# Cached attention on one core: two K blocks to the transposing DMA, a new list of K blocks turned by VectorE, and the first query projection in two row halves

## The chip, the cores and the metric

The kernel runs on one core of a Trainium2 chip. The metric is device time in microseconds (us) of one execution; the median over the executions shown is what is compared. Engines are named as the profile names them: PE (TensorE matmuls), PEld (its weight loads), DVE (VectorE), ACT (ScalarE), POOL (GpSimd), SP (the queue that issues most transfers).

## The reference, cut to what matters

```python
B, Sq, D = 8, 32, 1024;  Hq, Hkv, Sk, Dh = 32, 4, 8192, 128      # all bf16
W, rep = 2048, 8                                                  # W = Sk // 4; rep = Hq // Hkv
q = (x @ wq).reshape(B, Sq, Hq, Dh).transpose(0, 2, 1, 3)
k = repeat(k_cache[:, :, Sk-W:, :], rep, axis=1);  v likewise
p = softmax(einsum("bhqd,bhkd->bhqk", q, k) * Dh**-0.5)
out = einsum("bhqk,bhkd->bhqd", p, v).transpose(0, 2, 1, 3).reshape(B, Sq, Hq*Dh) @ wo
```

Only the last 2048 positions of the cache are used. There are 4 groups of 8 query heads; a group shares one K and one V of each batch row.

## The kernel before, in words

**Units and slots.** The work is 32 *units*, one for each pair of group and batch row, group by group: unit u is group u // 8 and batch row u % 8. A unit has 256 query rows (8 heads of 32 rows) against 2048 keys. It is done in four *slots* of 512 keys, so slot s belongs to unit s // 4, and there are 128 slots. In a slot PE makes the scores of this slot (`s_ps`, 4 matmuls of 256 columns), then the product with V of the slot two before (`o_ps`, 8 matmuls of 129 columns; the last of the 129 sums the softmax's denominator), and then whatever side work is planned for the slot. ACT takes the exponential of each slot's scores (`pT`) in one instruction. PE's stream is in exactly this order, so a score matmul that has to wait holds back all that stands behind it.

**Side work of PE.** It is put into slots by `side_plan`: the query projection of groups 1 to 3 (`q_pieces`, 16 pieces of 4 matmuls of 256 columns for each group, spread over `Q_SLOTS`), the output projection (`o_pieces`, over `O_SLOTS`), and, for the units in `PE_T`, the turning of K (`k_pieces`: 16 PE transposes of 128x128 for a unit, 4 in each slot of the unit before). The projection of group 0 is done in `start`, before the first score: for the first `Q_CUT` = 6 of the 8 pieces of the contraction on all 256 rows, for the last two on 128 rows; the other 128 rows of those two follow in slots 0 and 1 (`q_rest`). The pieces of `q_pieces` and of `k_pieces` share the two PSUM buffers of `ps_m`.

**Three ways to turn K.** The scores need K with the head dimension on the partitions. Units in `PE_T` (0 to 4) load K as it is and turn it on PE, with a copy out of PSUM by DVE. Units in `V_T` load K as it is (`k_raw`), DVE turns it in blocks of 32x32 (`kb`, four instructions), and then sixteen moves of blocks put it in place (`kTv`), all by POOL, except for unit 5, where DVE makes four of them. A score matmul of such a unit reads what all sixteen moves have written. All other units load K by a transposing DMA in two halves (`kT`, 256 KB each). An entry of `V_T` gives the unit in whose `load_unit` the load is issued, the slots of the four DVE blocks, and the first and last slot over which the moves are spread:

```python
V_T = {5: (2, (5, 6, 8, 10), 10, 17, 12),
       **{u: (u - 4, range(4 * u - 16, 4 * u - 12), 4 * u - 13, 4 * u - 4, 16) for u in (8, 11, 14, 17, 20, 23, 26, 29)}}
```

**Loads.** Nearly every transfer is issued by SP, in the order of `load_unit`, into one queue: for a unit the first half of K, V, the second half of K, and then the raw K of a later unit and the weights that `W_AT` assigns. Units 0 to 3 are issued in `start`, 4 to 7 at slot 8, unit u from 8 on at slot 4(u - 5). These slots only order the stream: SP itself waits for buffers and for room in the queue, not for slots. DVE also works in program order: at a unit's start it copies V beside the column of ones (`va_copy`, L409), two slots into the next unit it normalises the last one's result and turns it (`finish_unit`: L415, L420, L422), and it makes the casts of the query pieces (L278) and the blocks of `V_T` (L251) where the plan puts them. The raw K of `V_T` units is in four buffers, the turned K of those units in two (`kvt`, shared with the raw K of units 0 and 1), `kb` in two, V in six.

Of the kernel before, what the change touches and what calls it, by code (L numbers as in the profile page):

```python
# [11 lines left out]
BF16 = mybir.dt.bfloat16  # L12
FP32 = mybir.dt.float32
# [2 lines left out]

RL_LIMIT = 1.0e22
RL_MIN = 1.0e-10
Q_CUT = 6
N_WARM = (8, 0, 0)  # L20
VA_ROW = 160
V_HALVES = 30

PE_T = (0, 1, 2, 3, 4)

V_T = {5: (2, (5, 6, 8, 10), 10, 17, 12),
       **{u: (u - 4, range(4 * u - 16, 4 * u - 12), 4 * u - 13, 4 * u - 4, 16) for u in (8, 11, 14, 17, 20, 23, 26, 29)}}
W_AT = (3, 3, 4, 4, 8, 8, 9, 9, 11, 12, 13, 13, 14, 15, 16, 16, 18, 19, 19, 20, 22, 22, 23, 24, 25, 26, 28, 28)

Q_SLOTS = {1: (17, 31), 2: (38, 54), 3: (69, 83)}  # L30
O_SLOTS = {0: (54, 71), 1: (84, 101), 2: (99, 123), 3: (124, 143)}


# [71 lines left out]
class Fast:  # L105
# [101 lines left out]
    def load_unit(self, ui):  # L207

        if ui < len(self.units):
            if ui not in V_T:  # L210
                self.load_k(ui, None if ui in PE_T else 0)
            self.load_v(ui, self.nc.sync)
            if ui not in V_T and ui not in PE_T:
                self.load_k(ui, 1)
        for u, at in V_T.items():
            if at[0] == ui:
                self.load_k(u)
        for p, at in zip(self.weights, W_AT):
            if at == ui:
                p()  # L220

    def k_pieces(self, ui):

        if ui not in PE_T:
            return []
# [39 lines left out]
    def q_pieces(self, g):  # L267
        nc, P, DC = self.nc, self.P, self.DC
        st = {}

        def piece(hl, i):
            if i == 0:
                st["ps"] = self.ps_m.tile([P, 512], FP32, name="q_ps", tag="m")
            for c in range(i * DC // 2, (i + 1) * DC // 2):
                nc.tensor.matmul(st["ps"][:, 0:self.NQ], lhsT=self.wq_t[g, i][:, c % (DC // 2), hl * P:(hl + 1) * P],  # L275
                                 rhs=self.xT[:, c, :], start=(c == 0), stop=(c == DC - 1))
            if i == 1:
                nc.vector.tensor_copy(out=self.q_view(g)[:, :, hl, :],  # L278
                                      in_=st["ps"][:, 0:self.NQ].rearrange("p (b s) -> p b s", b=self.B))
        return [lambda h=h, i=i: piece(h, i) for h in range(self.rep) for i in range(2)]  # L280

    def o_pieces(self, g, t, cuts=(512, 512), st=None):

# [28 lines left out]
    def start(self):  # L312
        nc, P = self.nc, self.P
        warm = self.ps_s.tile([P, 512], FP32, name="warm_ps", tag="s_ps")
        one = nc.const_aps.tensor
        x_sb = self.vp.tile([P, self.NT, self.D], BF16, name="x_sb", tag="v")
        xf = self.x.rearrange("b s d -> (b s) d")
        H = self.DC // 2

        nc.sync.dma_start(out=x_sb[:, 0, :], in_=xf[0:P, :])  # L320
        nc.scalar.dma_start(out=x_sb[:, 1, :], in_=xf[P:2 * P, :])
        wq0 = self.load_wq(0, 0, (1, 1, 1, 1)) + self.load_wq(0, 1, (2, 1, 1))
        for p in wq0[:5]:
            p()
        self.load_k(0, 0)
        wq0[5]()
        wq0[6]()
        self.load_k(0, 1)
        self.load_v(0, nc.sync)
        self.load_k(1)  # L330
        self.load_v(1, nc.sync)
        self.weights = []
        for g in range(self.Hkv):
            if g + 1 < self.Hkv:
                self.weights += self.load_wq(g + 1, 0) + self.load_wq(g + 1, 1)
            if g:
                self.weights += self.load_wo(2 * g - 2) + self.load_wo(2 * g - 1)
        self.weights += self.load_wo(2 * self.Hkv - 2) + self.load_wo(2 * self.Hkv - 1)
        for ui in range(2, 4):
            self.load_unit(ui)  # L340
        for v in self.va:
            nc.gpsimd.memset(v[:, :, self.Dh:self.VW], 1.0)
        nc.gpsimd.memset(self.ones_c[:, :], 1.0)
        def warm_up(n):
            for i in range(n):
                nc.tensor.matmul(warm[:, :], lhsT=one(1.0, [P, P], BF16), rhs=one(1.0, [P, 512], BF16), start=True, stop=True)
        warm_up(N_WARM[0])


        def x_turn(half, pl, tag):  # L350
            ps = pl.tile([P, H, self.NT, P], BF16, name="xT_ps", tag=tag)
            for c in range(H):
                for t in range(self.NT):
                    nc.tensor.transpose(ps[:, c, t, :], x_sb[:, t, half * H + c:self.D:self.DC], self.ident[:, :])
            for i, copy in ((0, nc.vector.tensor_copy), (1, nc.scalar.copy)):
                c0 = half * H + i * H // 2
                copy(out=self.xT[:, c0:c0 + H // 2, :], in_=ps[:, i * H // 2:(i + 1) * H // 2, :, :].rearrange("p c t s -> p c (t s)"))

        x_turn(0, self.ps_m, "m")
        x_turn(1, self.ps_s, "s_ps")  # L360
        qs = [pl.tile([P, 2, self.NQ], FP32, name="q0_ps", tag=tag)
              for pl, tag in ((self.ps_o, "o_ps"), (self.ps_o, "o_ps"), (self.ps_m, "m"), (self.ps_m, "m"))]
        KT = self.KT
        tp = None

        def k_turn(half):
            for j in range(half * KT // 2, (half + 1) * KT // 2):
                nc.tensor.transpose(tp[:, j, :], self.k_raw[0][:, j, :], self.ident[:, :])

        def k_copy(half):  # L370
            sl = slice(half * KT // 2, (half + 1) * KT // 2)
            nc.vector.tensor_copy(out=self.kT[0][:, sl, :], in_=tp[:, sl, :])

        def q_mm(c, h, n0, n1):
            nc.tensor.matmul(qs[h // 2][:, h % 2, n0:n1], lhsT=self.wq_t[0, c // H][:, c % H, h * P:(h + 1) * P],  # L375
                             rhs=self.xT[:, c, n0:n1], start=(c == 0 and h % 2 == 0), stop=(c == self.DC - 1),
                             skip_group_check=True)

        for c in range(self.DC):
            for h in range(self.rep):  # L380
                q_mm(c, h, 0, P if c >= Q_CUT else self.NQ)
            if c == 0:
                warm_up(N_WARM[2])
                warm_sb = self.c1.tile([P, 8], BF16, name="warm_sb")
                nc.vector.tensor_copy(out=warm_sb[:, :], in_=warm[:, 0:8])
            if c == self.DC - 3:
                tp = self.ps_s.tile([P, KT, P], BF16, name="kf_ps", tag="s_ps")
                k_turn(0)
                k_copy(0)
        k_turn(1)  # L390

        def q_copy(eng, k, b0, b1):
            src = qs[k][:, :, :].rearrange("p h (b s) -> p b h s", b=self.B)[:, b0:b1, :, :]
            dst = self.q_view(0)[:, b0:b1, k * 2:(k + 1) * 2, :]
            (nc.vector.tensor_copy if eng == "v" else nc.scalar.copy)(out=dst, in_=src)
        for k, eng in ((0, "a"), (1, "v"), (2, "a"), (3, "v")):
            q_copy(eng, k, 0, 1)
        k_copy(1)
        self.va_copy(0)

        def q_rest(k):
            for h in (2 * k, 2 * k + 1):
                for c in range(Q_CUT, self.DC):
                    q_mm(c, h, P, self.NQ)
            q_copy("v", k, 1, self.B)
        self.q_rest = [lambda k=k: q_rest(k) for k in (0, 2, 3, 1)]

    def va_copy(self, ui):
        self.nc.vector.tensor_copy(out=self.va[ui % 3][:, :, 0:self.Dh], in_=self.v_sb[ui][:, :, :])  # L409
# [16 lines left out]
    def side_plan(self):  # L426

        S = self.B * self.NCH
        plan = {s: [] for s in range((len(self.units) + 8) * self.NCH)}

        def spread(pieces, s0, s1):
            for k, p in enumerate(pieces):
                plan[s0 + (s1 - s0) * k // len(pieces)].append(p)
        for g, w in Q_SLOTS.items():
            spread(self.q_pieces(g), *w)
        for g, w in O_SLOTS.items():
            spread(self.o_pieces(g, 0) + (self.o_pieces(g, 1) if g < self.Hkv - 1 else []), *w)
        for ui, (_, s0, s1, s2, _) in V_T.items():
            blocks, moves = self.kv_pieces(ui)
            for k, p in enumerate(blocks):  # L440
                plan[s0[k]].append(p)
            spread(moves, s1, s2)
        return plan

    def run(self):
        nc, P, NCH, CJ, UQ, QT_N, KT = self.nc, self.P, self.NCH, self.CJ, self.UQ, self.QT_N, self.KT
        self.start()
        plan = self.side_plan()
        for i, p in enumerate(self.q_rest):
            plan[i // 2].append(p)  # L450
        pv_queue = []

        loads = {8: [4, 5, 6, 7], **{4 * (u - 5): [u] for u in range(8, len(self.units))}}
# [202 lines left out]
```

## Time and profile before

| what | value |
|---|---|
| median of 14 runs | 185.96 us (185.38 to 187.82) |
| the profiled execution | 185.7 us, of which its span is 183.6 us and 2.1 us lie around it |
| first score matmul | 12.74 us after the span's start |
| last exponential ends | 174.4 us |
| PE busy / DVE / ACT / POOL | 97% / 63% / 72% / 52% of the span |
| DMA: read from HBM | 41.4 MB |
| granted PE clock | full throughout |

Times in this text count from the start of the profiled span. The page gives for each engine its busy time, and a row of digits for 40 equal slices of the span (4.6 us each), where 9 means a slice busy to 90% or more. A timeline view lists instructions in order of time, neighbours of one kind put together (x8), with the time from the first one's start to the last one's end; matmuls overlap, so a group's time is longer than the distance to the next group, and it is the distance that counts.

### The profile page before, as it was taken

To read this page: it belongs to the slowest core of one execution; us is meant where nothing else is said; L and a number is where in the kernel's file an instruction comes from. 1 tells how busy PE (TensorE), PEld (TensorE's weight loads), DVE (VectorE), ACT (ScalarE), POOL (GpSimd) and SP (SyncE) were. 2 spreads that over 40 slices of the span, in tenths; PEclk is the share of its full clock that TensorE was granted. 3 is DMA by queue.
4 is the path that set the end of the run, shared out by engine and by line. 5 is a ranking of instruction groups with operands and counts; after the bars stand their busy time and mean duration, and the time that the engine had idled before them with its cause. 6 is when DMAs were issued, how large, how long until landed. Compare 5 with 4: busy or idle time off the path is not lost.

```text
span 183.6 us, 5041 instructions
## 1 busy us (share of the span) xinstructions
PE 178.9 (97%) x2041; PEld 153.6 (84%) x2057; DVE 115.5 (63%) x266; ACT 131.6 (72%) x133; POOL 95.0 (52%) x150
## 2 busy tenths in 40 slices
PE   8999999999999999999999999999999999999994
PEld 2899989999999999987878999988787888888843
DVE  0248799996585785685557558647755865365363
ACT  2218898777889787878787677787877888888800
POOL 2000019749939959929954980796299279600000
PEclk9999999999999999999999999999999999999999
DMA  6999999899998989999999999999999999960003
GB/s 192 341 404 409 399 402 379 125 276 385 258 355 264 347 289 326 400 253 255 365 366 241 374 398 239 241 345 385 245 369 335 209 284 291 225 172 0 0 29 93
DMA packets 52953, 51.72 MB, mean 282 GB/s; under 512 B 39744, under 2 KB 40256, under 8 KB 52928
## 3 DMA queue, kind: packets, MB, share of 16 engines
q1 hardware_dynamic: 52352, 50.90, 97.5%
q10 hardware_dynamic: 576, 0.49, 0.8%
q8 instruction: 15, 0.25, 0.5%
q14 instruction: 10, 0.08, 0.1%
HBM read 41.42 MB, written 0.52 MB: 228 GB/s over the span
## 4 chain that ended last, share of the span: by engine, by line
PE 83%; DMA 14%; SPq 1%; issue 1%; DVE 0%
PE o_ps L478 29%; PE s_ps L467 28%; PE op_ps L295 14%; PE q_ps L275 11%; DMA k_raw<-in_k_cache_dram 6%; DMA v_sb<-in_v_cache_dram 5%; DMA wq_sb<-in_wq_dram 3%; SPq L164 1%; PE tp L236 1%; SPq L320 0%; DVE o_t L305 0%; PE cnt_ps L532 0%
## 5 line engine op out<-in xcount | busy, mean ns | idle before, releaser
L469 ACT ACTIVATE pT<-s_ps 128x1024 bf16<-128x1024 f32 x128 | 128.8, 1025 | 33.0 <-PE s_ps L467 32.1
L261 POOL TENSOR_SCALAR kTv<-kb 32x512 bf16<-32x512 bf16 x140 | 94.1, 672 | 64.0 <-PE s_ps L467 34.6
L478 PE MATMUL o_ps<-va,pT 128*128 128x129 bf16 x1024 | 78.8, 220 | 0.1
L478 PEld LDWEIGHTS <-pT 128*128 128x128 bf16 x1024 | 68.5, 98 | 3.1
L467 PE MATMUL s_ps<-QT,kT 128*128 128x256 bf16 x368 | 55.2, 272 | 0.2
L467 PEld LDWEIGHTS <-kT 128*128 128x128 bf16 x368 | 34.8, 98 | 10.3
L295 PE MATMUL op_ps<-wo_sb,OT 128*128 128x512 bf16 (+2 forms) x128 | 32.7, 352 | 0.6
L275 PE MATMUL q_ps<-xT,wq_sb 128*128 128x256 bf16 x192 | 28.2, 273 | 0.0
L409 DVE COPY va<-v_sb 128x2048 bf16<-128x2048 bf16 x32 | 25.4, 795 | 0.1
L251 DVE STREAM_TRANSPOSE kb<-k_raw 128x512 bf16<-128x512 bf16 x36 | 23.8, 685 | 0.0
L415 DVE RECIPROCAL RL_all<-o_ps 128x2 f32<-128x2 f32 x32 | 5.3, 165 | 28.0 <-PE o_ps L478 27.9
L467 PE MATMUL s_ps<-QT,kTv 128*128 128x256 bf16 x144 | 21.6, 272 | 0.0
L420 DVE TENSOR_SCALAR o_sb<-o_ps,RL_all 128x128 bf16<-128x128 f32 x64 | 19.5, 347 | 1.1
L467 PEld LDWEIGHTS <-kTv 128*128 128x128 bf16 x144 | 13.9, 98 | 5.1
L275 PEld LDWEIGHTS <-wq_sb 128*128 128x128 bf16 x192 | 17.0, 98 | 1.2
L278 DVE CAST QT<-q_ps 128x256 bf16<-128x256 f32 x24 | 9.8, 407 | 12.8 <-PE q_ps L275 12.8
L422 DVE STREAM_TRANSPOSE OT<-o_sb 128x256 bf16<-128x256 bf16 x32 | 14.3, 446 | 1.1
L295 PEld LDWEIGHTS <-OT 128*128 128x128 bf16 x144 | 11.4, 98 | 2.3 <-DVE OT L422 0.2
L302 DVE TENSOR_TENSOR oacc<-op_ps,oacc 128x512 f32<-128x512 f32 x8 | 5.5, 682 | 7.4 <-PE op_ps L295 7.4
L375 PE MATMUL q_ps<-xT,wq_sb 128*128 128x256 bf16 (+1 forms) x80 | 7.7, 251 | 0.0
L375 PEld LDWEIGHTS <-wq_sb 128*128 128x128 bf16 x80 | 6.6, 98 | 0.9 <-issue 0.2
L236 PE MATMUL tp<-ident,k_raw 128*128 128x128 bf16 x64 | 5.9, 219 | 0.2 <-DMA k_raw<-in_k_cache_dram 0.2
(30 smaller groups left out, 36.8 us busy)
## 6 DMA issues: line engine op xcount, KB each, us to landing
v_sb<-in_v_cache_dram SPq DMA_DIRECT2D x30, 512.0 KB, 7.2
wo_sb<-in_wo_dram SPq DMA_DIRECT2D x16, 512.0 KB, 6.3
wq_sb<-in_wq_dram SPq DMA_DIRECT2D x13, 512.0 KB, 7.3
k_raw<-in_k_cache_dram SPq DMA_DIRECT2D x13, 512.0 KB, 5.7
wq_sb<-in_wq_dram SPq DMA_DIRECT2D x6, 256.0 KB, 5.0
v_sb<-in_v_cache_dram SPq DMA_DIRECT2D x4, 256.0 KB, 5.0
kT<-in_k_cache_dram SPq DMA_TRANSPOSE x36, 6.6
k_raw<-in_k_cache_dram SPq DMA_DIRECT2D x2, 256.0 KB, 6.4
```

Of the source, the lines that this page charges most:

```text
L251: nc.vector.transpose(out=st["kb"][:, sl, :], in_=self.k_raw[ui][:, sl, :])
L261: nc.gpsimd.tensor_scalar(out=out, in0=in_, scalar1=1.0, scalar2=1.0, op0=ALU.mult, op1=ALU.mult)
L275: nc.tensor.matmul(st["ps"][:, 0:self.NQ], lhsT=self.wq_t[g, i][:, c % (DC // 2), hl * P:(hl + 1) * P], rhs=self.xT[:, c, :], start=(c == ...
L278: nc.vector.tensor_copy(out=self.q_view(g)[:, :, hl, :], in_=st["ps"][:, 0:self.NQ].rearrange("p (b s) -> p b s", b=self.B))
L295: nc.tensor.matmul(ps[:, 0:w], lhsT=self.OT[:, gq, c, t * P:(t + 1) * P], rhs=self.wo_t[gq][:, c, n0:n0 + w], start=(k == 0), stop=(k == 7))
L375: nc.tensor.matmul(qs[h // 2][:, h % 2, n0:n1], lhsT=self.wq_t[0, c // H][:, c % H, h * P:(h + 1) * P], rhs=self.xT[:, c, n0:n1], start=(c ...
L409: self.nc.vector.tensor_copy(out=self.va[ui % 3][:, :, 0:self.Dh], in_=self.v_sb[ui][:, :, :])
L420: nc.vector.tensor_scalar(out=o_sb[:, qt, :, :], in0=o_ps[:, qt, 0:Dh].rearrange("p (i c) -> p c i", c=4), scalar1=rl[:, ui * QT_N + qt:ui ...
L422: nc.vector.transpose(out=self.OT[:, g * QT_N:(g + 1) * QT_N, :, b * self.Sq:(b + 1) * self.Sq], in_=o_sb[:, :, :, :])
L467: nc.tensor.matmul(s_ps[:, jj, :], lhsT=self.kT[ui][:, c * CJ + jj, :], rhs=q_u, start=True, stop=True)
L469: nc.scalar.activation(out=pT[:, :, :], in_=s_ps[:, :, :], func=ACT.Exp, bias=0.0, scale=self.scale)
L478: nc.tensor.matmul(o_ps[:, qt, 0:self.VW], lhsT=pT[:, jj, qt * P:(qt + 1) * P], rhs=va[:, j, 0:self.VW], start=(j == 0 and qt == 0), stop= ...
```

## The change

Units 3 and 4 leave `PE_T`; their K comes by transposing DMA. `V_T` now has units 5, 9, 11, 13, 16, 18, 21, 23, 26 and 29 in place of 5, 8, 11, 14, 17, 20, 23, 26 and 29. So 19 units use the transposing DMA in place of 18, 13 load raw K in place of 14. In `load_unit` the weights now come ahead of the raw K of a later unit. In the projection of group 0, heads 0 to 3 are done on all 256 rows before the first score, heads 4 to 7 on the first 128 rows only; the second 128 rows of these four heads are done by `q_late`, two heads in slots 0 and 1, two in slots 8 and 10. The first turn of K0 on PE moves behind the sixth of the eight contraction pieces. The projection of group 1 starts in slot 14 in place of 17 (one piece in each of the slots 14 to 29), four heads at a time on their first half of the contraction and then on their second. In all later groups two heads share one PSUM buffer and one cast.

```diff
-PE_T = (0, 1, 2, 3, 4)
+PE_T = (0, 1, 2)
 V_T = {5: (2, (5, 6, 8, 10), 10, 17, 12),
-       **{u: (u - 4, range(4 * u - 16, 4 * u - 12), 4 * u - 13, 4 * u - 4, 16) for u in (8, 11, 14, 17, 20, 23, 26, 29)}}
+       9: (5, range(21, 25), 24, 32, 16),
+       **{u: (u - 4, range(4 * u - 16, 4 * u - 12), 4 * u - 13, 4 * u - 4, 16) for u in (11, 13, 16, 18, 21, 23, 26, 29)}}
-Q_SLOTS = {1: (17, 31), 2: (38, 54), 3: (69, 83)}
+Q_LATE = {0: (0, 2), 1: (8, 12)}
+Q_SLOTS = {1: (14, 31), 2: (38, 54), 3: (69, 83)}
...
     def load_unit(self, ui):
...
+        for p, at in zip(self.weights, W_AT):
+            if at == ui:
+                p()
         for u, at in V_T.items():
             if at[0] == ui:
                 self.load_k(u)
-        for p, at in zip(self.weights, W_AT):
-            if at == ui:
-                p()
...
     def q_pieces(self, g):
...
+        n = 4 if g == 1 else 2
+        return [lambda h=h, i=i: piece(h, i) for h0 in range(0, self.rep, n) for i in range(2) for h in range(h0, h0 + n)]
+
+    def q_late(self, h0):
...
+            for c in range(DC):
+                nc.tensor.matmul(st["ps"][:, i, :], lhsT=self.wq_t[0, c // (DC // 2)][:, c % (DC // 2), (h0 + i) * P:(h0 + i + 1) * P],
+                                 rhs=self.xT[:, c, P:self.NQ], start=(c == 0 and i == 0), stop=(c == DC - 1), skip_group_check=True)
             if i == 1:
+                nc.vector.tensor_copy(out=self.q_view(0)[:, B // 2:, h0:h0 + 2, :].rearrange("p b h s -> p h b s"),
+                                      in_=st["ps"][:, :, :].rearrange("p h (b s) -> p h b s", b=B // 2))
...
-        def q_mm(c, h, n0, n1):
+        def q_mm(c, h):
+            ps, n = (qs[h // 2][:, h % 2, :], self.NQ) if h < 4 else (qs[2][:, h - 4, :], P)
...
         for c in range(self.DC):
-            for h in range(self.rep):
-                q_mm(c, h, 0, P if c >= Q_CUT else self.NQ)
...
-            if c == self.DC - 3:
+            if c == self.DC - 2:
                 tp = self.ps_s.tile([P, KT, P], BF16, name="kf_ps", tag="s_ps")
                 k_turn(0)
                 k_copy(0)
+            for h in range(self.rep):
+                q_mm(c, h)
...
-        for i, p in enumerate(self.q_rest):
-            plan[i // 2].append(p)
```

More of the change, by code (lines that the diff above doesn't have):

```diff
@@ L18 @@
 RL_MIN = 1.0e-10
-Q_CUT = 6
-N_WARM = (8, 0, 0)
+N_WARM = 8
 VA_ROW = 160
 V_HALVES = 30
-PE_T = (0, 1, 2, 3, 4)
+PE_T = (0, 1, 2)
 V_T = {5: (2, (5, 6, 8, 10), 10, 17, 12),
-       **{u: (u - 4, range(4 * u - 16, 4 * u - 12), 4 * u - 13, 4 * u - 4, 16) for u in (8, 11, 14, 17, 20, 23, 26, 29)}}
+       9: (5, range(21, 25), 24, 32, 16),
+       **{u: (u - 4, range(4 * u - 16, 4 * u - 12), 4 * u - 13, 4 * u - 4, 16) for u in (11, 13, 16, 18, 21, 23, 26, 29)}}
 W_AT = (3, 3, 4, 4, 8, 8, 9, 9, 11, 12, 13, 13, 14, 15, 16, 16, 18, 19, 19, 20, 22, 22, 23, 24, 25, 26, 28, 28)
-Q_SLOTS = {1: (17, 31), 2: (38, 54), 3: (69, 83)}
+Q_LATE = {0: (0, 2), 1: (8, 12)}
+Q_SLOTS = {1: (14, 31), 2: (38, 54), 3: (69, 83)}
 O_SLOTS = {0: (54, 71), 1: (84, 101), 2: (99, 123), 3: (124, 143)}
@@ L271, in piece @@
         def piece(hl, i):
+            k = hl // 2
+            if i == 0 and hl % 2 == 0:
+                st[k] = self.ps_m.tile([P, 2, self.NQ], FP32, name="q_ps", tag="m")
+            for c in range(i * DC // 2, (i + 1) * DC // 2):
+                nc.tensor.matmul(st[k][:, hl % 2, :], lhsT=self.wq_t[g, i][:, c % (DC // 2), hl * P:(hl + 1) * P],
+                                 rhs=self.xT[:, c, :], start=(c == 0 and hl % 2 == 0), stop=(c == DC - 1), skip_group_check=True)
+            if i == 1 and hl % 2 == 1:
+                nc.vector.tensor_copy(out=self.q_view(g)[:, :, 2 * k:2 * k + 2, :].rearrange("p b h s -> p h b s"),
+                                      in_=st[k][:, :, :].rearrange("p h (b s) -> p h b s", b=self.B))
@@ L272, in piece @@
+        n = 4 if g == 1 else 2
+        return [lambda h=h, i=i: piece(h, i) for h0 in range(0, self.rep, n) for i in range(2) for h in range(h0, h0 + n)]
+    def q_late(self, h0):
+        nc, P, DC, B = self.nc, self.P, self.DC, self.B
+        st = {}
+        def piece(i):
             if i == 0:
[L273 to L276, printed above, removed]
+                st["ps"] = self.ps_m.tile([P, 2, P], FP32, name="ql_ps", tag="m")
+            for c in range(DC):
+                nc.tensor.matmul(st["ps"][:, i, :], lhsT=self.wq_t[0, c // (DC // 2)][:, c % (DC // 2), (h0 + i) * P:(h0 + i + 1) * P],
+                                 rhs=self.xT[:, c, P:self.NQ], start=(c == 0 and i == 0), stop=(c == DC - 1), skip_group_check=True)
@@ L277, in piece @@
             if i == 1:
-                nc.vector.tensor_copy(out=self.q_view(g)[:, :, hl, :],
-                                      in_=st["ps"][:, 0:self.NQ].rearrange("p (b s) -> p b s", b=self.B))
-        return [lambda h=h, i=i: piece(h, i) for h in range(self.rep) for i in range(2)]
+                nc.vector.tensor_copy(out=self.q_view(0)[:, B // 2:, h0:h0 + 2, :].rearrange("p b h s -> p h b s"),
+                                      in_=st["ps"][:, :, :].rearrange("p h (b s) -> p h b s", b=B // 2))
@@ L282, in o_pieces @@
+        return [lambda i=i: piece(i) for i in range(2)]
     def o_pieces(self, g, t, cuts=(512, 512), st=None):
@@ L346, in warm_up @@
                 nc.tensor.matmul(warm[:, :], lhsT=one(1.0, [P, P], BF16), rhs=one(1.0, [P, 512], BF16), start=True, stop=True)
-        warm_up(N_WARM[0])
+        warm_up(N_WARM)
         def x_turn(half, pl, tag):
@@ L360, in start @@
         x_turn(1, self.ps_s, "s_ps")
-        qs = [pl.tile([P, 2, self.NQ], FP32, name="q0_ps", tag=tag)
-              for pl, tag in ((self.ps_o, "o_ps"), (self.ps_o, "o_ps"), (self.ps_m, "m"), (self.ps_m, "m"))]
+        qs = [self.ps_o.tile([P, 2, self.NQ], FP32, name="q0_ps", tag="o_ps") for _ in range(2)]
+        qs.append(self.ps_m.tile([P, 4, P], FP32, name="q0_ps", tag="m"))
         KT = self.KT
@@ L372, in k_copy, with q_copy @@
             nc.vector.tensor_copy(out=self.kT[0][:, sl, :], in_=tp[:, sl, :])
-        def q_mm(c, h, n0, n1):
-            nc.tensor.matmul(qs[h // 2][:, h % 2, n0:n1], lhsT=self.wq_t[0, c // H][:, c % H, h * P:(h + 1) * P],
-                             rhs=self.xT[:, c, n0:n1], start=(c == 0 and h % 2 == 0), stop=(c == self.DC - 1),
+        def q_mm(c, h):
+            ps, n = (qs[h // 2][:, h % 2, :], self.NQ) if h < 4 else (qs[2][:, h - 4, :], P)
+            nc.tensor.matmul(ps, lhsT=self.wq_t[0, c // H][:, c % H, h * P:(h + 1) * P],
+                             rhs=self.xT[:, c, 0:n], start=(c == 0 and h in (0, 2, 4)), stop=(c == self.DC - 1),
                              skip_group_check=True)
+        def q_copy(copy, h0, h1, b0, b1):
+            ps = qs[h0 // 2] if h0 < 4 else qs[2]
+            copy(out=self.q_view(0)[:, b0:b1, h0:h1, :].rearrange("p b h s -> p h b s"),
+                 in_=ps[:, :, b0 * self.Sq:b1 * self.Sq].rearrange("p h (b s) -> p h b s", s=self.Sq))
         for c in range(self.DC):
-            for h in range(self.rep):
-                q_mm(c, h, 0, P if c >= Q_CUT else self.NQ)
[L382 to L385, printed above, removed]
-            if c == self.DC - 3:
+            if c == self.DC - 2:
                 tp = self.ps_s.tile([P, KT, P], BF16, name="kf_ps", tag="s_ps")
@@ L389, in start @@
                 k_copy(0)
-        k_turn(1)
[L392 to L397, printed above, removed]
+            for h in range(self.rep):
+                q_mm(c, h)
+            if c == 0:
+                warm_sb = self.c1.tile([P, 8], BF16, name="warm_sb")
+                nc.vector.tensor_copy(out=warm_sb[:, :], in_=warm[:, 0:8])
+        k_turn(1)
+        q_copy(nc.scalar.copy, 0, 2, 0, 1)
+        q_copy(nc.vector.tensor_copy, 2, 4, 0, 1)
+        q_copy(nc.scalar.copy, 4, 8, 0, 1)
         k_copy(1)
         self.va_copy(0)
[L401 to L406, printed above, removed]
+        q_copy(nc.vector.tensor_copy, 0, 2, 1, self.B)
+        q_copy(nc.vector.tensor_copy, 2, 4, 1, self.B)
+        q_copy(nc.vector.tensor_copy, 4, 8, 1, self.B // 2)
     def va_copy(self, ui):
@@ L433, in spread @@
                 plan[s0 + (s1 - s0) * k // len(pieces)].append(p)
+        for k, w in Q_LATE.items():
+            spread(self.q_late(4 + 2 * k), *w)
         for g, w in Q_SLOTS.items():
```

## The prediction

> **What bounds the kernel now.** I read the page's first part, the rows of its second part, the chain, and then timelines of single engines.
>
> ```profile
> PE 178.9 (97%) x2041; PEld 153.6 (84%) x2057; DVE 115.5 (63%) x266; ACT 131.6 (72%) x133; POOL 95.0 (52%) x150
> ...
> DMA  6999999899998989999999999999999999960003
> ...
> PE 83%; DMA 14%; SPq 1%; issue 1%; DVE 0%
> ...
> L261 POOL TENSOR_SCALAR kTv<-kb 32x512 bf16<-32x512 bf16 x140 | 94.1, 672 | 64.0 <-PE s_ps L467 34.6
> ```
>
> PE never rests, and the chain is PE but for the first 28 us; side work taken from PE should therefore shorten the span. The DMA row is the warning: the transfers run without a rest from 3 to 164 us. POOL's average of 52% looks harmless, but it is one stage's business, so I read it as a timeline:
>
> ```profile
> 27.05 8.72 POOL L261 TENSOR_SCALAR kTv<-kb 32x512 bf16<-32x512 bf16 x12 [25.48 <-PE s_ps L467]
> 39.08 11.72 POOL L261 TENSOR_SCALAR kTv<-kb 32x512 bf16<-32x512 bf16 x16 [3.30 <-PE o_ps L478]
> 53.59 11.69 POOL L261 TENSOR_SCALAR kTv<-kb 32x512 bf16<-32x512 bf16 x16 [2.79 <-DVE kb L251]
> 67.26 11.68 POOL L261 TENSOR_SCALAR kTv<-kb 32x512 bf16<-32x512 bf16 x16 [1.98 <-DVE kb L251]
> ```
>
> A unit's sixteen moves are one train of **11.7 us**, whatever unit it is. PE's pace beside them:
>
> ```profile
> 28.96 0.60 PE L467 MATMUL s_ps<-QT,kT 128*128 128x256 bf16 x4
> 29.40 0.62 PE L478 MATMUL o_ps<-va,pT 128*128 128x129 bf16 x8
> 29.85 0.39 PE L236 MATMUL tp<-ident,k_raw 128*128 128x128 bf16 x4
> 30.07 0.60 PE L467 MATMUL s_ps<-QT,kT 128*128 128x256 bf16 x4
> ```
>
> Start to start, the scores take 0.44, the product with V 0.45, four K transposes 0.22: a slot of 1.11. A slot with a query piece (0.44) is 1.33, so a unit takes 5.3 us where every slot has one; a slot without side work is 0.905, ACT's own pace (scores start at 53.30, 54.21, 55.13). Three units apart is 15.9 us, two units apart 10.6: less than one train.
>
> **What the Trainium skill says.** (1) Perfetto Trace Analysis, "Identifying the Most-Contended Engine": the busy share of matmuls overstates how full PE is, weight loads tell more. They are 84% here, but the start-to-start distances above leave no room either, so the trace sides with a full PE. (2) TensorE: Matmul & The Clock Gate, "Wait — 56ns, not 53.3ns?": 55.6 ns for a warm matmul of 128 columns; the trace agrees (0.22 us for four). (3) DMA: Bandwidth & Descriptors, "Latency and other measured facts": a contiguous DMA transpose runs at 350 to 400 GB/s. The trace differs: worked out below, a half of 256 KB costs 1.57 us, 167 GB/s, and I take that. (4) GPSIMD Engine Reference, "Key points": it shares its SBUF interfaces with VectorE and contends with it. The trains last 11.3 to 12.0 us in all later units under differing DVE load, so I take 11.7 and no surcharge.
>
> **The change part by part.**
>
> *Transposes off PE.* 32 x 0.0556 = **-1.78**. Also gone is the late K4: its transposes start at 27.61 where 27.22 was due, **-0.39**. The four PSUM copies (0.67 each) leave DVE, which has slack there: 0.
>
> *First projection.* Before the first score each of the 8 contraction steps has 1536 columns; before it had 2048 in six steps and 1024 in two. That is 0.85 less in all. But steps arrive by DMA: landings are 9.10 for steps four and five, 10.60 for six, 11.29 for seven, and 11.96 for K0's second half. Walking through these, with 0.64 a step and 0.44 for eight transposes, the first score comes at 12.6 for 12.74: **-0.15**. The rest moves into slots: 16 matmuls of 0.0556 more than before, **+0.88**. Slots 9, 11, 12, 13 and 30 become bare and fall to ACT's pace, 0.02 each: +0.1. The query pieces of group 1 are moved, not changed. K1's transposes in slot 2 may wait for the last query copy on DVE (three of about 0.6 after V's copy at 14.2, so 16.0 for 15.46): up to +0.5, which the wait in slot 18 below swallows. Fewer, wider casts (about 0.69 for 512 elements, extended from 0.407 for 256 and 0.616 for 448) lie beside PE: 0. Sum on PE: -1.78 - 0.39 - 0.15 + 0.88 + 0.1 = **-1.3**, if nothing is late.
>
> *The queue of transfers.* The trace has each transfer's landing. From V5's landing (34.14) to the last half of K31 (164.55) are 57 transfers of 512 KB and 36 transposed halves. At 1.30 for the former (ten of them land from 20.84 to 34.14), 130.4 - 74.1 leaves 56.3, so 1.57 a half; bounds are 0.8 and 2.6, the shortest and longest distances between landings. A transposed K thus costs 3.1 for 1.3. Up to the second half of group 1's weights the queue gains four halves and loses raw K3, K4 and K8: +2.4, landing at 35.2 for 32.81. First use is in slot 18, about 34.4: PE waits 0.6 to 0.9, and unit 5 starts at **36.6** (before: 36.49), the gain used up. Up to K10's first half it is four halves more than before and one plain transfer less, +5.0 (57.45 + 5.0), while counting on from 20.84 gives 61.6: I take **62.0**. Its matmuls would be due at 59.6 and came at 60.53 before: unit 10 is 1.5 late against before. V9 lands at 56.4 to 57.1, its copy is used at 57.4: nothing or 0.4. In total the queue grows by 2 x 1.57 - 1.30 = 1.8 and ends at 166.4; K31's second half is needed at 171.3: hidden. SP is only moved with it: the room in the queue paces it before and after, and raw K8's 2.5 us wait for a buffer goes.
>
> *Three trains, two units apart.* The last DVE block of K9 stands behind this on DVE: the product of slot 19 ends in slot 21 at 39.0; `finish_unit` 1.28 (39.43 to 40.71 before), cast 0.69, three blocks 1.95, V's copy 0.8, block 0.69: 44.4. POOL begins **44.5** (bounds 43.9 and 45.0: unit 5 half a us earlier, or the copy waiting for V6). Then trains stand one behind another, since each successor's blocks are done before (K11 lands at 47.8, K13 at 60.3): K9 44.5 to 56.2, K11 to 67.9, K13 to **79.6**. PE wants K9 at 55.2, so it waits 1.1; K11 at 67.3 after unit 10's delay, wait 0.7; K13 at 67.9 + 10.6 = 78.5, wait 1.1. Unit 13's first score comes at 79.7, before it was 76.45: **+3.2**. K13's raw load now stands behind two weight transfers and lands at 60.3, with its first block due on DVE at 57. Behind it wait `finish_unit` of unit 8 and V10's copy, which ends at 65.05, just as PE wants it in slot 42 (65.1). So this costs nothing, with no margin.
>
> *After unit 13.* PE has the same pieces in the same slots as before, at the same price, so the lateness stays. Trains have room: K16 starts at about 80.4 and is done at 92.1, needed at 95.6; K18 at 103.8 for 106.9; later ones as before. Transfers lead by 3 us or more.
>
> The sum: the span becomes 183.6 + 3.2 = 186.8, the execution 185.7 + 3.2 = 188.9. The profiled execution was 0.26 under the median (185.96 + 3.2 = 189.2); I say **189.0**. A measurement of this kernel can tell about 0.5% from no change.
>
> **The rivals.** *A, faster:* PE's -1.3 comes through, 184.5. For it, PE 97% busy and a chain of PE. It asks that K13's train be done by 75.1, hence that the first of three begins at 40.0, before slot 24's DVE block can even be reached: trains of 11.3 instead of 11.7 give 78.4, still late. It wins only if trains overlap or shorten in a way no train shows. *B, the queue alone:* trains are no limit, K10 is: +1.5, 187.3; at 0.8 a half it would be on time. Against it is only POOL's sum. *C, both add:* halves cost 2.0 or more, K13 lands after 62, DVE stands still under it, V10's copy comes at 67 or later, and blocks that start then push the train behind: +4.5 to +5.5, 190.7. For it: no margin above.
>
> **How the numbers follow.** Forecast 0.72 (own range 187.8 to 190.0: the start 43.9 to 45.0 and three trains of 11.34 to 11.97 against 11.7), B 0.09, C 0.12, A 0.07. The range 187.0 to 190.8 takes in B and most of C. Faster by over 0.5% is A, 0.07; within 0.5% 0.04, a little of B with short halves; slower 0.89.
>
> **What would show it.** Right: POOL's timeline shows the trains of K9, K11 and K13 as one block of 35 us from about 44.5; PE idles about 3 us before scores of units 9, 11 and 13, released by POOL, and about 1 us on K10's DMA; unit 13 starts near 79.7; PE's busy time falls by 1 us while the span grows by 3. Wrong: unit 13 before 77, or idle time of PE after unit 13.

## The result and the profile after

The changed kernel takes **189.31 us** (median of 10 runs, 188.23 to 191.18) against 185.91 beside it: 1.0167 of the time before, with a 95% interval of 1.0138 to 1.0196, 3.4 us more between the medians. The ratios here and below leave out runs that fell in a slower state, such as 191.18 of this kernel and 189.55 of the one with short trains, and are not the quotients of the medians. The forecast was 189.0. The profiled execution took 189.93 us with a span of 187.2.

The page's first part, the DMA row, the chain and POOL's row, as before:

```profile
PE 178.3 (95%) x2025; PEld 151.8 (81%) x2041; DVE 114.3 (61%) x254; ACT 131.2 (70%) x133; POOL 104.9 (56%) x166
...
DMA  5999999999999999999999999999999999950012
...
PE 72%; POOL 16%; DMA 4%; issue 3%; DVE 2%; SPq 1%
...
L262 POOL TENSOR_SCALAR kTv<-kb 32x512 bf16<-32x512 bf16 x156 | 104.0, 666 | 57.2 <-DVE kb L252 39.8
```

PE works 0.6 us less (the forecast was 1), and the span is 3.6 us longer. POOL is busy for 56% on average, hardly more than before, but it has entered the chain with 16%, where it had no share at all. POOL's timeline shows where:

```profile
27.91 8.71 POOL L262 TENSOR_SCALAR kTv<-kb 32x512 bf16<-32x512 bf16 x12 [26.34 <-DVE kb L252]
44.57 34.95 POOL L262 TENSOR_SCALAR kTv<-kb 32x512 bf16<-32x512 bf16 x48 [7.96 <-PE s_ps L482]
80.04 23.24 POOL L262 TENSOR_SCALAR kTv<-kb 32x512 bf16<-32x512 bf16 x32 [0.52 <-DVE kb L252]
```

Before, there were separate lines of x16 with idle time between. Now the trains of K9, K11 and K13 are one line of x48: 34.95 us without a gap, from 44.57 to 79.52. PE's timeline has the other end of it, at the first scores of the three units and at unit 10's product:

```profile
56.81 0.61 PE L482 MATMUL s_ps<-QT,kTv 128*128 128x256 bf16 x4 [0.84 <-POOL kTv L262]
...
61.44 0.61 PE L482 MATMUL s_ps<-QT,kT 128*128 128x256 bf16 x4
...
64.91 0.61 PE L493 MATMUL o_ps<-va,pT 128*128 128x129 bf16 x8 [0.21 <-DVE va L424]
...
68.45 0.61 PE L482 MATMUL s_ps<-QT,kTv 128*128 128x256 bf16 x4 [1.16 <-POOL kTv L262]
...
79.58 0.61 PE L482 MATMUL s_ps<-QT,kTv 128*128 128x256 bf16 x4 [0.34 <-POOL kTv L262]
```

The idle time in brackets understates a wait, since a group's modelled end reaches into it: start to start, unit 9 is 1.0 us late, unit 11 1.3, unit 13 0.5. Unit 13 starts 0.06 us after the last move, at 79.58 for 76.45 before: +3.1. Unit 31 starts at 172.25 for 169.11: +3.1 still. Nothing is lost or won in the 18 units between.

The span grew by 3.6 us, and 0.4 of it lies behind all this: from the landing of the last output to the end of the span it is 1.33 us (185.90 to 187.23) for 0.90 before (182.75 to 183.65). In the eight profiles of kernels that turn fewer than five K blocks on PE this stretch is 1.26 to 1.34, in the four others 0.90 to 0.96. No experiment was made on it, and its cause stays open.

### The profile page after: what moved, and what is told of

Read it like the earlier page. It is cut to its first block, busy times and chain, and to the rows that moved or that the text cites. A ratio compares the mean times of both kernels' runs of the same rounds, so it can differ in the third digit from the quotient of the medians.

```text
span 187.2 us, 5014 instructions
## 1 busy us (share of the span) xinstructions
PE 178.3 (95%) x2025; PEld 151.8 (81%) x2041; DVE 114.3 (61%) x254; ACT 131.2 (70%) x133; POOL 104.9 (56%) x166
## 4 chain that ended last, share of the span: by engine, by line
PE 72%; POOL 16%; DMA 4%; issue 3%; DVE 2%; SPq 1%
PE o_ps L493 24%; PE s_ps L482 23%; POOL kTv L262 16%; PE op_ps L313 14%; PE q_ps L277 7%; DMA wq_sb<-in_wq_dram 4%; PE q_ps L394 2%; PE tp L237 1%; SPq L165 1%; DVE QT L400 1%; PE kf_ps L386 0%; PE ql_ps L293 0%; DVE kT L390 0%; DVE va L424 0%; SPq L338 0%
## 5 line engine op out<-in xcount | busy, mean ns | idle before, releaser
L484 ACT ACTIVATE pT<-s_ps 128x1024 bf16<-128x1024 f32 x128 | 128.4, 1024 | 35.5 <-PE s_ps L482 35.2
L262 POOL TENSOR_SCALAR kTv<-kb 32x512 bf16<-32x512 bf16 x156 | 104.0, 666 | 57.2 <-DVE kb L252 39.8
L482 PE MATMUL s_ps<-QT,kT 128*128 128x256 bf16 x352 | 52.8, 273 | 0.0
L482 PEld LDWEIGHTS <-kT 128*128 128x128 bf16 x352 | 33.3, 98 | 10.3 <-DMA kT<-in_k_cache_dram 0.3
L252 DVE STREAM_TRANSPOSE kb<-k_raw 128x512 bf16<-128x512 bf16 x40 | 26.2, 684 | 7.1 <-DMA k_raw<-in_k_cache_dram 7.1
L482 PE MATMUL s_ps<-QT,kTv 128*128 128x256 bf16 x160 | 24.0, 273 | 2.4 <-POOL kTv L262 2.3
L482 PEld LDWEIGHTS <-kTv 128*128 128x128 bf16 x160 | 15.2, 98 | 8.5 <-POOL kTv L262 3.1
L277 PEld LDWEIGHTS <-wq_sb 128*128 128x128 bf16 x192 | 16.9, 98 | 1.1
L280 DVE CAST QT<-q_ps 128x512 bf16<-128x512 f32 x12 | 8.0, 668 | 6.6 <-PE q_ps L277 6.6
L394 PE MATMUL q_ps<-xT,wq_sb 128*128 128x256 bf16 (+1 forms) x64 | 6.0, 246 | 1.2 <-DMA wq_sb<-in_wq_dram 1.2
L394 PEld LDWEIGHTS <-wq_sb 128*128 128x128 bf16 x64 | 5.0, 98 | 2.1 <-DMA wq_sb<-in_wq_dram 1.6
L323 DVE TENSOR_TENSOR o_t<-op_ps,oacc 128x512 bf16<-128x512 f32 (+2 forms) x6 | 3.1, 513 | 3.7 <-remote 2.1
```

What stands on the lines that cost most here:

```text
L252: nc.vector.transpose(out=st["kb"][:, sl, :], in_=self.k_raw[ui][:, sl, :])
L262: nc.gpsimd.tensor_scalar(out=out, in0=in_, scalar1=1.0, scalar2=1.0, op0=ALU.mult, op1=ALU.mult)
L277: nc.tensor.matmul(st[k][:, hl % 2, :], lhsT=self.wq_t[g, i][:, c % (DC // 2), hl * P:(hl + 1) * P], rhs=self.xT[:, c, :], start=(c == 0 a ...
L280: nc.vector.tensor_copy(out=self.q_view(g)[:, :, 2 * k:2 * k + 2, :].rearrange("p b h s -> p h b s"), in_=st[k][:, :, :].rearrange("p h (b ...
L394: nc.tensor.matmul(ps, lhsT=self.wq_t[0, c // H][:, c % H, h * P:(h + 1) * P], rhs=self.xT[:, c, 0:n], start=(c == 0 and h in (0, 2, 4)), ...
L482: nc.tensor.matmul(s_ps[:, jj, :], lhsT=self.kT[ui][:, c * CJ + jj, :], rhs=q_u, start=True, stop=True)
```

## The experiments

Ten kernels ran, each with the kernel before beside it, in five rounds. The times are medians.

| kernel | us | ratio to before, 95% interval | first score of unit 13 |
|---|---|---|---|
| changed kernel | 189.31 | 1.0167 [1.0138, 1.0196] | 79.58 |
| new list alone | 188.87 | 1.0158 [1.0132, 1.0183] | 79.71 |
| changed, old list | 187.98 | 1.0104 [1.0075, 1.0134] | 77.47 |
| changed, K3 and K4 on PE | 191.48 | 1.0294 [1.0270, 1.0319] | 82.11 |
| changed, half of K9's moves on DVE | 189.61 | 1.0208 [1.0170, 1.0246] | 80.02 |
| changed, short trains | 187.83 | 1.0115 [1.0074, 1.0155] | 77.86 |
| new list alone, short trains | 185.68 | 0.9998 [0.9974, 1.0023] | 76.48 |
| changed, short trains, plain K3 and K4 | 185.97 | 1.0004 [0.9982, 1.0026] | 75.66 |
| changed, old load order | 188.86 | 1.0196 [1.0165, 1.0227] | 78.72 |
| changed, K9 one slot later | 191.36 | 1.0331 [1.0295, 1.0367] | 81.64 |
| before, K4 alone by DMA | 185.75 | 1.0010 [0.9993, 1.0028] | 75.95 |

The **trains theory** says that the three trains set unit 13. Its rival, the **queue theory**, says that the transposing DMA of K3 and K4 does, by making later transfers late.

### The list by itself, and the change without it

To the kernel before, only this was done:

```diff
-       **{u: (...) for u in (8, 11, 14, 17, 20, 23, 26, 29)}}
+       9: (5, range(21, 25), 24, 32, 16),
+       **{u: (...) for u in (11, 13, 16, 18, 21, 23, 26, 29)}}
```

> The kernel before with nothing but the new list of VectorE units (5, 9, 11, 13, 16, ...). Trains theory: K9's train starts at about 45.0, the three trains end near 80, unit 13 starts 3.5 us later than before: 189.4. Queue theory: K3 and K4 load as before, K10's first half lands at 57.45 + 1.3 = 58.7, before it is due at 60.5: 185.9, as before.

Measured: 188.87, 2.8 us more than the 186.1 beside it. K3 and K4 load as before, so the queue theory's "as before" falls: **the list alone costs nearly all that the whole change costs**. Its POOL timeline is the changed kernel's, beginning 0.5 us later:

```profile
45.09 34.56 POOL L262 TENSOR_SCALAR kTv<-kb 32x512 bf16<-32x512 bf16 x48 [8.91 <-PE o_ps L479]
```

The opposite, the changed kernel with the old list:

> The changed kernel with the old list of VectorE units (5, 8, 11, 14, 17, ...), all else of the change kept. Trains theory (three POOL trains of 11.7 us two units apart set unit 13): the trains of K8, K11 and K14 start at about 39, 54 and 67 and end before their units, so no score waits for POOL; K10's first half lands 1.3 us earlier than in the changed kernel (no raw K13 ahead of it), 60.1, when it is due. Unit 13 starts at 76.2 instead of 79.6: 3.4 us less, 185.9; 185.0 if the first score comes at 12.7 as before instead of 13.7. Queue theory (the transposing DMA of K3 and K4 is what costs the time): those are still there, so at least 187.5.

Measured: 187.98. That is less than the changed kernel, and no score waits for POOL for more than 0.3 us, but it is 1.9 us above before: the trains theory by itself, with its 185.9, misses by 2 us. DVE's timeline shows what I had overlooked:

```profile
32.22 0.58 DVE L259 COPY kTv<-kb 32x512 bf16<-32x512 bf16 x1
36.34 0.71 DVE L251 STREAM_TRANSPOSE kb<-k_raw 128x512 bf16<-128x512 bf16 x1 [3.53 <-DMA k_raw<-in_k_cache_dram]
...
40.53 0.65 DVE L423 COPY va<-v_sb 128x2048 bf16<-128x2048 bf16 x1
```

Raw K8 stands behind the transposed halves of K3 and K4 and, in the new order of `load_unit`, also behind two weight transfers, and landed at 36.31, against 30.14 before. DVE stood for 3.5 us at its first block, and the copy of V5, next in its order, came at 40.53 instead of the slot's 36.5. PE's first product of unit 5 waited for it: unit 6 starts 6.9 us after unit 5 instead of 5.3. So late landings have a price of their own, paid through DVE's program order. This run doesn't say how much of it is the transposing DMA's: the two weights landed at 32.26 and 33.60, behind K4's last half at 30.87, so the new order alone is an estimated 2.7 of the 6.2 us. It is also a price of the old list, as the new one has no raw K8.

### The trains cut short

```diff
+            if ui in (9, 11, 13):
+                if d == 0:
+                    nc.gpsimd.tensor_scalar(out=self.kT[ui][:, :, k * 32:(k + 1) * 32], in0=st["kb"][:, :, k * 32:(k + 1) * 32],
+                                            scalar1=1.0, scalar2=1.0, op0=ALU.mult, op1=ALU.mult)
+                return
```

First in the kernel with the list alone:

> The kernel before with the new list alone, and the trains of units 9, 11 and 13 cut to four POOL instructions in the same way (placing across partitions left out). Trains theory: the 2.8 us that the list alone cost go away whole, 186.0, since K10's first half lands at about 59 and is due at 60.5. If the list's cost lay in its loads or in DVE's blocks: 188.9 stays.

Measured: 185.68, ratio 0.9998. All loads and DVE blocks of the new list are still there, and the cost is gone whole. **What the list costs are the trains.** Then in the changed kernel:

> The changed kernel with the trains of units 9, 11 and 13 cut to four POOL instructions of 128 partitions each. They touch all of the turned K but leave out the placing of the blocks across partitions, so these units compute with a wrongly ordered K; loads, DVE and PE keep their instructions. Trains theory with the queue behind it: trains of 2.7 us end long before units 9, 11 and 13; what is left is K10's landing at 61.4 and V10's copy, so unit 13 starts at 61.4 + 5.3 + 0.4 + 10.6 = 77.7 instead of 79.6 and the time is 187.4. If trains were all that is late: the PE sum's -1.3 comes through, 184.6. If they are not the cause: 189.3.

Measured: 187.83. The waits for POOL are gone, and the expected second limit stands in their place in PE's timeline, K10's first half, which landed at 61.52:

```profile
61.56 0.61 PE L487 MATMUL s_ps<-QT,kT 128*128 128x256 bf16 x4 [0.92 <-DMA kT<-in_k_cache_dram]
...
65.03 0.61 PE L498 MATMUL o_ps<-va,pT 128*128 128x129 bf16 x8 [0.21 <-DVE va L429]
```

That this rest is the queue's was tested by taking the transposition out of the loads of K3 and K4 as well:

```diff
+            if ui in (3, 4):
+                nc.sync.dma_start(out=self.kT[ui][:, part * H:(part + 1) * H, :],
+                                  in_=src.rearrange("(p j) d -> p j d", j=KT)[:, part * H:(part + 1) * H, :])
+                return
```

> The changed kernel with the trains of units 9, 11 and 13 cut as in the run with short trains, and with K3 and K4 loaded into the same buffers by plain transfers of the same halves (these two units compute with an unturned K, the three others with a wrongly ordered one). If trains and queue are all there is: four halves at 0.65 instead of 1.48, K10's first half at about 58.1, due at 59.9; nothing waits, unit 13 starts at 75.9 and the time is 185.2, which is the PE sum with the first score at 13.2. If something else of the change costs the 2 us that short trains left: 187.8 stays.

Measured: 185.97, ratio 1.0004: nothing of the loss is left. K10's first half lands at 59.31, and the scores of unit 10, at 59.70, do not wait. Up to unit 13, trains and queue are all there is on the loss side. But the gain that I expected under them, 185.2, isn't measured either; more on that below.

### Where the trains begin

> The changed kernel with K3 and K4 turned on PE again, new list kept. Trains theory: PE does 32 transposes more ahead of unit 5, so DVE's last block of K9 and with it the trains come 1.75 us later; unit 13 starts at about 81.3 and the time is 189.3 + 1.7 = 191.0. Queue theory: the queue is 3.5 us shorter at K10, nothing is late, and the time returns to 186 to 187.

The edit is `PE_T = (0, 1, 2, 3, 4)`. Measured: 191.48. Taking the load off the queue made it slower, as only the trains theory had it. PE reached unit 5 at 39.92 instead of 37.14, more than the 1.75 us of the expectation, because the pieces of `q_late`, of group 1's projection and of `k_pieces` now contend for the two buffers of `ps_m` in units 2 and 3: PE waits there three times for DVE's copy of the turned K (`kT`), for 0.18, 0.85 and 0.62 us. The first train began at 47.35.

> The changed kernel with K9's four DVE blocks and its moves one slot later in the plan. The last block then stands behind the result of unit 5 on DVE, so the trains start at about 47.0 instead of 44.6. Trains theory: the whole 2.4 us reach the end, 191.7. If the trains had any slack, or the queue set unit 13: less, down to 189.3.

The edit is `9: (5, range(22, 26), 25, 33, 16)`. Measured: 191.36, 2.05 us above the changed kernel. The first train began at 46.49, 1.9 later. Two side effects were not foreseen. With K9's moves ending in slot 32, two of K11's, planned for slot 31, come ahead of K9's last two on POOL, so unit 9 waited until 59.63. And after these 4.0 us without a matmul PE ran at half its clock for 3.4 us. In the view by stretches the granted clock is the third number from the end:

```profile
55.60:59.60 4.00, 0.00 (x0) 0.00 (x0) 0.81 (x1) 0.70 (x1) 3.66 (x6) 1.00 1.47 367
59.60:63.03 3.43, 3.40 (x24) 2.92 (x25) 0.71 (x1) 1.58 (x2) 3.07 (x6) 0.51 0.79 226
63.03:70.00 6.97, 6.97 (x85) 6.49 (x84) 5.37 (x14) 5.49 (x6) 6.39 (x10) 1.00 1.06 290
```

The first two slots of unit 9 took 3.4 us, where scores and products at 0.44 and 0.45 make 1.8. From there PE's pace set unit 13, at 81.64, with the third train done 0.5 us ahead, at 81.10. By estimate unit 13 would have been due at 80.0 without these 1.6 us, and the train would have set it, 1.6 us later than in the changed kernel. So the result fits the trains theory, but unit 13 didn't wait for the third train here, and the run is no measure of how much of a later start comes through. The five kernels in which unit 13 did wait are that:

| kernel | first train starts | third ends | unit 13 starts |
|---|---|---|---|
| old load order | 43.98 | 78.66 | 78.72 |
| half of K9's moves on DVE | 44.51 | 79.96 | 80.02 |
| changed kernel | 44.57 | 79.52 | 79.58 |
| new list alone | 45.09 | 79.65 | 79.71 |
| K3 and K4 on PE | 47.35 | 82.05 | 82.11 |

In each of them the score follows the last move by 0.06 us.

### Relief that gave none

> The changed kernel with 8 of K9's 16 moves on DVE instead of POOL. Trains theory: K9's train shrinks from 11.7 to 5.4 us, K11's starts at 53.9 when its last block is done, K13's ends at 77.1. Then K10's landing at 61.4 is the last to bind (61.4 + 5.3 + 0.4 + 10.6 = 77.7): unit 13 1.9 us earlier, 187.4. If POOL doesn't bind: no change, 189.3, or a little more from the load on DVE.

The edit is `9: (5, range(21, 25), 24, 32, 8)`. Measured: 189.61, no gain; the expectation was wrong. K9's part on POOL did shrink, to 5.32 us, but DVE was too full for the other eight moves. They stand between K11's blocks, so K11's last block ended at 56.34 instead of 53.84 and its train began only at 56.52:

```profile
44.51 5.32 POOL L262 TENSOR_SCALAR kTv<-kb 32x512 bf16<-32x512 bf16 x8 [8.55 <-PE s_ps L482]
56.52 23.44 POOL L262 TENSOR_SCALAR kTv<-kb 32x512 bf16<-32x512 bf16 x32 [6.69 <-DVE kb L252]
```

POOL lay idle for 6.7 us waiting for DVE, and the last move ended at 79.96. Two direct waits came on top: a score behind a late query cast (0.94) and a product behind the late copy of V8 (1.37).

> The changed kernel with the old order in load_unit: raw K of a later unit ahead of the weights. K13 lands at about 57.9 instead of 60.5, DVE's wait for it shrinks from 4.3 to about 1.7 us. Trains theory: K13's train can't start before K11's has ended, so nothing changes, 189.3. If DVE's wait for K13 is what makes unit 11 and 13 late: 1 to 2 us less.

The edit puts the two loops of `load_unit` back in their old order. Measured: 188.86; its interval overlaps the changed kernel's. Unit 13 came 0.9 us earlier in its profile, but the first train also began 0.6 earlier, with a first score at 13.11 instead of 13.70, and the score again follows the third train. DVE's long wait for K13 in the new order (4.33 us) costs nothing that shows, as the trains theory has it.

> The kernel before with K4 alone moved to the transposing DMA, and with group 1's query pieces in the changed order from slot 14 on; old list, old first projection, old load order. PE loses 16 transposes (0.89) and the wait for the late K4 (0.39) and gains nothing. The queue grows by 1.8 us: K10's first half at about 59.3, due at 59.2; trains keep their distance of three units. So -1.2: 184.8. If a longer queue always costs what it grows: 186 to 187.

This was the version meant to beat both kernels. Measured: 185.75, ratio 1.0010, interval 0.9993 to 1.0028: a tie with before. Unit 13 starts at 75.95 and unit 31 at 168.61, each 0.5 us ahead of before, less than a measurement tells apart. The expected 1.2 us did not come: the first score came at 13.09 for 12.74, and unit 11 lost another 0.2 us, its score starting 0.06 us after its train's last move. I have found no version that is measurably faster than before.

## Why the prediction was right, point by point

- **The three trains: right, and shown.** The prediction had K9's last block ending at 44.4, the trains from 44.5 to 79.6 and unit 13 at 79.7; the trace has 44.42, 44.57 to 79.52 and 79.58. Two agreements hide misses. The product of slot 19 was there for DVE at 39.56, not 39.0, since unit 5 was late, and DVE's chain from there to the block took 4.9 us, not the 5.4 summed; that these cancel is luck. Single trains took 12.19, 11.55 and 11.05 for 11.7 each, which cancels in their sum; the last section shows where the difference comes from. That the trains are the cause is shown by the list alone (+2.8) and by its return to before with short trains.
- **The queue's price: right in the landings, one reading off.** The queue ended at 166.8 for 166.4. The ten plain transfers of the prediction, from 20.84 to 34.14, give 1.33 us each, not 1.30, so a half is 54.6 / 36 = 1.52 us in the kernel before. In the changed one, from V5's landing (36.78) to K31's last half (166.81) lie 59 transfers of 512 KB and 34 halves: 130.0 - 59 x 1.33 = 51.6, or 1.52 again. K10's first half landed at 61.40 for 62.0, V10's copy ended at 64.86 for 65.05. But PE stood only 0.2 us before K10's scores, not the forecast 1, as unit 9 was itself late; unit 10 came 0.9 us later than before, for 1.5. The 350 to 400 GB/s of the Trainium skill (DMA: Bandwidth & Descriptors, "Latency and other measured facts") would have priced a half at 0.7 us, as an estimate, and missed this; in this stream of mixed transfers the 167 GB/s worked out from the landings (172 with 1.52 us) decides.
- **How the two combine: right.** Alone, the list costs 2.8 us. The rest of the change costs 1.9 with the old list, through raw K8, and 2.0 with the new list and short trains, through K10. Together they cost 3.4, not 4.7 or so. In the changed kernel the late K10 falls into time in which unit 11 would wait for POOL anyway. Rival B (187.3) is what the run with short trains shows (187.83); rival C did not happen.
- **The first score: wrong in size, with hardly an effect on the total.** Forecast 12.6, measured 13.70. The step that failed was to take one execution's landing as fixed and to see a gain behind it. In all twelve profiles PE starts on steps four and five of the contraction, counted from zero, 0.04 to 0.05 us after they land, and the first score comes 3.6 us later. They landed at 9.10 in the profile before, at 10.04 in the changed kernel's, and at 8.91 to 9.63 in the ten others; why it varies stays open. What is left to do then is the same in both orders, 6144 columns and the sixteen transposes of K0 (whose first eight stand behind the sixth piece before as well as after). The columns that the split puts off all lie ahead of this landing, and there PE now waits longer, 1.15 us in the changed kernel. The forecast -0.15 came for the most part from pricing a step at 0.64, where it takes 0.67. So the split gains nothing: with the new first projection the first score lies at 12.57 to 13.70, mean 13.1 of eight, with the old one at 12.74 to 13.18, mean 13.0 of four.
- **Unit 5: 37.14 for 36.6**, but not for the reason given. The weights landed at 34.03, not 35.2, and PE did not wait for them in slot 18; the late first score did it.
- **Unit 11's wait: 1.3 us for 0.7**, since PE got to it earlier (67.1) and K11's train ended later (68.39) than forecast; unit 13's was 0.5 for 1.1, unit 9's 1.0 for 1.1. The trains' end is the same.
- **PE's sum of -1.3: mis-sized.** With trains and queue removed, the time is 185.97 for 185.67 beside it. In that profile unit 13 is 0.8 us ahead of before (75.66 for 76.45) and unit 31 only 0.5 (168.65 for 169.11), with 0.3 lost in unit 20. The last 0.5 goes at the end of the span, which is 183.66 for 183.65: the stretch behind the last output, a cost that the sum did not have, takes 0.4 of it. The term of the sum itself that failed is the first score: 13.01 where -0.15 on 12.74 was counted, 0.4 lost. Rival A would not have come to 184.5 even with the trains out of the way.

## What to carry to other kernels

Average load says little about a helper engine: add up the time of one job there and compare it with the distance between two jobs' due times where they are closest. A job of 11.7 us every 15.9 us is hidden; the same job three times at 10.6 us is a new critical path, though POOL is 44% idle. When work is taken off the bounding engine, price what feeds it in its own queues, and read late landings through the engines that wait in program order: with the old list a late raw K cost nothing itself, but the V copy queued behind it on DVE did. And before work is moved out of a stage that waits for data, ask on which side of the wait it lies: what stands ahead of the landing was free.

## What the runs showed of the hardware that I had not expected

A POOL move of 128 partitions by 512 elements took a median of 0.620 us, one of 32 partitions by 512 elements 0.612, in the same profile (short trains with plain K3 and K4). Four times the partitions cost next to nothing; the two differ in one thing more, as the narrow ones also shift their block to other partitions:

```profile
L271 POOL TENSOR_SCALAR kTv<-kb x108: 607/612/1046, 27.3 to 158.5; 32x512 bf16<-32x512 bf16 x108
L265 POOL TENSOR_SCALAR kTv<-kb x12: 615/620/1049, 44.0 to 64.4; 128x512 bf16<-128x512 bf16 x12
```

Within a train most moves are 0.61 us with 0.06 between, 10.7 us for sixteen. The rest comes from single long moves, and each of these runs beside a V copy on DVE. Two lines of the changed kernel's timeline show one, in K9's train:

```profile
48.57 0.68 DVE L424 COPY va<-v_sb 128x2048 bf16<-128x2048 bf16 x1
48.60 1.12 POOL L262 TENSOR_SCALAR kTv<-kb 32x512 bf16<-32x512 bf16 x1
```

In this profile 24 of the 156 moves take 0.86 to 1.12 us. All 24 overlap a V copy, and each V copy that meets a train lengthens one move. The other 132 take at most 0.63, though many stand beside DVE's transposes and casts. In the twelve profiles it is 283 of 284 moves over 0.7 us. K9's train met three V copies, K11's two, K13's one: 12.19, 11.55 and 11.05 us. So point (4) of the prediction left something out: "Key points" of the GPSIMD Engine Reference in the Trainium skill limits the contention with VectorE to certain of its instructions, those in a 2-port mode or with two SBUF inputs, and not every DVE instruction lengthens a move here. No trace shows in which mode the V copies ran. The 11.7 us needed no surcharge because the trains that it was read from had met three copies each. That the copy is the cause is read from these overlaps; no run moved the copies away.

The half clock after PE's rest, shown above for K9 one slot later, is the other thing. In the eleven other profiles the longest distance between the starts of two matmuls, from the first score to 170 us, is 1.9 us, and none of them shows the clock fall in this stretch.
